# A gated mix of a long convolution and an MLP mixer: the DFT split 32 x 64 on halves of the PE array, with other transposes and another order of work

## The chip, the cores and the metric

The kernel runs on one core of one Trainium2 chip. The metric is the time of one execution on the device in microseconds (us): 305.72, the median of three runs (305.12 to 305.99). A core has TensorE (PE, with its weight loads as PEld), VectorE (DVE), ScalarE (ACT), GpSimd (POOL) and SyncE (SP), which here issues all DMAs. Each runs its own instructions in order and waits for the others at semaphores.

## The reference

Two branches over a sequence of S = 2048 rows of D = 640 channels, in bf16, mixed by a gate for each row. Branch A multiplies a 4-tap shifted k by v, convolves the product with a 2048-tap filter per channel, adds a direct term, and multiplies by q. Branch B is an MLP mixer on the same x (A_q): layer norm, w1, gelu, shifts of the four channel groups by +1, -1, +2, -2 rows, w2, a residual, layer norm, w3, gelu, w4, a residual.

```python
g = sigmoid((x * gate_w).sum(-1, keepdims=True))
k_shift = sum(k_pad[:, t:t + S, :] * shift_k[:, 3 - t] for t in range(4))
kv = k_shift * v
y = irfft(rfft(pad(kv, 2 * S)) * rfft(pad(ssm_k, 2 * S)))[:, :S] + kv * ssm_D
a = q * y
h = gelu(layernorm(x) @ w1)
x1 = x + shift_groups(h, (1, -1, 2, -2)) @ w2
b = x1 + gelu(layernorm(x1) @ w3) @ w4
out = g * a + (1 - g) * b
```

## The kernel before

**Layout.** A tile of 128 partitions holds the rows t = 16 t2 + t1 with t2 on the partitions and t1 = 0..15 as 16 slots of 640 channels. X (later X1, in place) and KV hold all 2048 rows in this way.

**Branch B.** `load_x` brings a quarter of x, `x_transpose` turns it with one DMA transpose of 20 blocks (L460), `x_stats` gets the norm, `mlp1` (L509, L510) does w1 and gelu for one slot into hr, which is laid out by channel group. `h_dma` then issues five DMA transposes for a quarter: one for each channel group (L516, into HT, padded by 16 columns) and one for the rest (L517, into HM0). `h_mixed` shifts HM0 into HM with four DMAs and small DVE copies. `w2` (L554) reads the shifted blocks, adds into X on DVE (L558) and squares on ACT (L560). `x1_norm` and a DMA transpose (L578) give x1t, `w3` (L596, gelu L597) and `w4` (L604) follow. w4 adds its PSUM to X1 on DVE; the four last ones write the result.

**Branch A.** `kv_load` and `kv_compute` (DVE, L432 to L438) form KV. `h_transpose` turns the filter ssm_k on PE into HT0. The DFT of length 4096 is done in steps. `step1` multiplies by F1 (128 x 256, its halves hf = 0, 1), 1024 columns a PSUM tile, evicted by ACT (L323) and written to the scratch S_h or S_x in DRAM. `gather` reads the scratch with rows and columns exchanged, `step2` multiplies by the table T2 (32 groups), `product` multiplies the two spectra on DVE (L357 to L359), `step3` multiplies by I1 and I2 and writes S_g, `gin` reads it back exchanged, and `step4` (L616) adds both halves of F4 and combines with q, the gate and X1 on DVE (L621 to L628). The tables T2, I1, I2 are spread out by POOL (L240) out of CMP. All evictions of step1, step2 and step3 are ACT's.

**What sets the order.** Every piece is put into a list with a time, and the list is sorted; up to time 45 the order of SP's instructions is that of the list, the rest is left to the scheduler of the framework. Pools limit what can run ahead: PSUM has two pools of two buffers, psc (branch A) and psm (branch B); hr, xn and a few others share two "row" buffers; HT0, the tables and W1N share one place (tag RT), W3 and the first part of ssm_k another.

Of the kernel before, what the change touches and what calls it, by code (L numbers as in the profile page):

```python
# [20 lines left out]
NT = 16  # L21
NG = 32
# [4 lines left out]
HS = 160  # L27
HPAD = 16
# [14 lines left out]
def kernel(  # L43
# [16 lines left out]
    nc = tc.nc  # L60
    V, A, G, PE, SP = nc.vector, nc.scalar, nc.gpsimd, nc.tensor, nc.sync

    q_rows = A_q.rearrange("b (t2 t1) d -> (b t2) t1 d", t1=NT)
    k_rows = A_k.rearrange("b (t2 t1) d -> (b t2) t1 d", t1=NT)
    v_rows = A_v.rearrange("b (t2 t1) d -> (b t2) t1 d", t1=NT)
    o_rows = out.rearrange("b (t2 t1) d -> (b t2) t1 d", t1=NT)
# [3 lines left out]
    PC = []  # L70
    n0 = 0
    for gi in range(4):
        PC.append((n0, 128, gi * 160))
        n0 += 128
    for gi in range(4):
        PC.append((n0, 32, gi * 160 + 128))
        n0 += 32

    tasks = []
    GTB = 4  # L80

    def add(t, fn):
        tasks.append((t, len(tasks), fn))
# [9 lines left out]
    S_h = [dram.tile([P, NT * D], BF16, name=f"S_h{i}") for i in range(2)]  # L93
    S_x = [dram.tile([P, NT * D], BF16, name=f"S_x{i}") for i in range(2)]
    S_g = [dram.tile([16, P, D], BF16, name=f"S_g{i}") for i in range(2)]
# [3 lines left out]
    F1 = const.tile([P, 256], BF16, name="F1")  # L99
    F4 = const.tile([P, 2, P], BF16, name="F4")  # L100
    CMP = const.tile([P, 3, NG, 2, 16], BF16, name="CMP")
# [3 lines left out]
    R128 = const.tile([P, P], F32, name="R128")  # L105
# [9 lines left out]
    EX = G  # L115
# [45 lines left out]
    def load_x(c):  # L161
        SP.dma_start(out=X[:, 4 * c:4 * c + 4, :], in_=q_rows[:, 4 * c:4 * c + 4, :])
# [6 lines left out]
    def load_w2():  # L169
        for (nn, cnt, oo) in PC:  # L170
            kt, po = nn // P, nn % P
            SP.dma_start(out=W2P[po:po + cnt, kt, :], in_=B_w2[oo:oo + cnt, :])
# [10 lines left out]
    def consts0():  # L183
        G.iota(pi[:], pattern=[[0, 1]], base=0, channel_multiplier=1)
        G.iota(R128[:], pattern=[[1, P]], base=0, channel_multiplier=0, allow_small_or_imprecise_dtypes=True)
# [558 lines left out]
```

## Time and profile before

| | |
|---|---|
| median of the runs | 305.72 us |
| the profiled execution | 304.15 us, span of its instructions 302.3 us |
| PE busy | 242.2 us, 80% of the span |
| PEld busy | 121.2 us |
| DVE busy | 176.9 us, 58% |
| ACT busy | 179.1 us, 59% |
| POOL busy | 28.3 us |
| DMA | 62.50 MB, mean 207 GB/s |
| granted clock of PE, mean | 0.941 |

The page gives busy time of an engine, its share of the span, and the same in 40 slices of 7.6 us, in tenths. Matmuls overlap, so that a run of them has to be read from the start of one to the start of the next. A row of the timeline gives start, length, engine, line, operation, what is written from what, the number of instructions put together, and in brackets how long the engine was idle ahead of it and for whom. A row of the grouped lines gives shapes and count, busy time, mean length in ns of one, then idle time and for whom. The rows of the stretches give, for PE, PEld, DVE, ACT and POOL, busy us and count, then the clock, the share of DMA and GB/s.

### The profile page before, as it was taken

The numbers are of one execution on the slowest core, as the hardware profiler recorded it, in microseconds if no ns is written. First come the engines' busy times: TensorE is split into PE (matmuls) and PEld (weight loads), VectorE is DVE, ScalarE is ACT, GpSimd is POOL, SyncE is SP. The second block draws the span as 40 slices with busy tenths as digits, with TensorE's granted clock in tenths as the row PEclk, the third lists the DMA queues.
The fourth block names the chain that finished last, engine by engine and source line by source line (L and its number), as shares of the span: only waits on it lengthen the run. The fifth ranks groups of instructions, "written<-read, shape, count | busy, mean of one in ns | idle before, by whom it ended". The sixth has DMA issues, their size and how long they took to land.

```text
span 302.3 us, 3944 instructions
## 1 busy us (share of the span) xinstructions
PE 242.2 (80%) x1434; PEld 121.2 (40%) x1434; DVE 176.9 (58%) x344; ACT 179.1 (59%) x284; POOL 28.3 (9%) x31
## 2 busy tenths in 40 slices
PE   2058858364639888999999999999999999995585
PEld 1024535231205444444454445444445454453232
DVE  8767969927899876501125234462343724099983
ACT  1999867242626666997868886469793676400000
POOL 6011302000000211990000000000000000000000
PEclk9999998975968999999999999999999999999559
DMA  6999979585699299958975458554975021775511
GB/s 201 242 259 401 206 202 314 96 236 170 157 283 400 59 269 280 359 205 225 321 288 173 129 193 194 183 173 128 413 242 174 3 87 43 245 278 175 175 43 43
DMA packets 60307, 62.50 MB, mean 207 GB/s; under 512 B 34304, under 2 KB 51457, under 8 KB 60288
## 3 DMA queue, kind: packets, MB, share of 16 engines
q1 hardware_dynamic: 60288, 62.25, 67.2%
q8 instruction: 11, 0.18, 0.2%
q14 instruction: 8, 0.07, 0.1%
HBM read 35.55 MB, written 18.35 MB: 178 GB/s over the span
## 4 chain that ended last, share of the span: by engine, by line
PE 30%; DVE 22%; ACT 13%; SPq 7%; DMA 7%; issue 6%; POOL 1%; ACTq 0%; DVEq 0%; POOLq 0%
PE ps L604 9%; PE ps L596 8%; ACT xs L348 6%; SPq L516 5%; PE ps L321 3%; DVE hs L359 3%; DVE p L358 3%; DVE p L357 3%; PE ps L370 3%; DVE X L558 3%; ACT gs L374 3%; DVE ot L625 2%; ACT stg L323 2%; PE ps L372 2%; PE ps L346 2%
## 5 line engine op out<-in xcount | busy, mean ns | idle before, releaser
L604 PE MATMUL ps<-W,gt 128*128 128x512 bf16 (+1 forms) x384 | 62.5, 306 | 0.8 <-DVE ot L607 0.8
L596 PE MATMUL ps<-x1t,W 128*128 128x512 bf16 x240 | 59.0, 379 | 0.0
L323 ACT CAST stg<-ps 128x1024 bf16<-128x1024 f32 x40 | 38.4, 1020 | 20.5 <-PE ps L321 10.4
L509 PE MATMUL psm<-WA,xt 128*128 128x512 bf16 (+1 forms) x160 | 30.0, 348 | 20.3 <-DVE WA L455 10.2
L604 PEld LDWEIGHTS <-gt 128*128 128x128 bf16 x384 | 30.2, 99 | 24.8 <-issue 3.7
L610 DVE TENSOR_TENSOR X<-ps,X 128x640 bf16<-128x640 f32 x12 | 9.9, 823 | 47.9 <-PE ps L604 47.9
L596 PEld LDWEIGHTS <-W 128*128 128x128 bf16 x240 | 22.3, 97 | 25.2
L357 DVE TENSOR_TENSOR p<-xs,hs 64x2560 bf16<-64x2560 bf16 x8 | 11.9, 1487 | 33.2 <-ACT xs L348 33.2
L374 ACT CAST gs<-ps 128x640 bf16<-128x640 f32 x32 | 20.6, 695 | 16.7 <-PE ps L372 14.5
L597 ACT ACTIVATE gt<-ps 128x1024 bf16<-128x1024 f32 x24 | 24.6, 1027 | 8.0 <-PE ps L596 7.7
L509 PEld LDWEIGHTS <-xt 128*128 128x128 bf16 x160 | 14.9, 111 | 32.0 <-issue 18.5
L346 PE MATMUL ps<-ax,TB 128*128 128x512 bf16 (+1 forms) x128 | 26.2, 298 | 0.3
L554 PE MATMUL psw<-WA,HT 128*128 128x512 bf16 (+1 forms) x128 | 22.4, 306 | 4.6 <-DVE X L558 3.6
L348 ACT CAST xs<-ps 128x640 bf16<-128x640 f32 x32 | 20.2, 696 | 9.0 <-PE ps L346 8.9
L321 PE MATMUL ps<-HT,F 128*128 128x512 bf16 x40 | 13.4, 441 | 13.9 <-ACT stg L323 7.2
L348 ACT CAST hs<-ps 128x640 bf16<-128x640 f32 x32 | 20.3, 696 | 0.1
L464 POOL TENSOR_TENSOR rs<-ve,EXPO 128x4 f32<-128x4 f32 x8 | 10.3, 1290 | 106.7 <-DVE ve L572 70.3
L437 DVE TENSOR_TENSOR acc<-acc,tmp 128x1280 bf16<-128x1280 bf16 x24 | 19.7, 823 | 0.5
L432 DVE TENSOR_TENSOR tmp<-K,cj 128x1280 bf16<-128x1280 bf16 (+1 forms) x25 | 19.8, 794 | 0.4
L510 ACT ACTIVATE hr<-psm,rs 128x640 bf16<-128x640 f32 x16 | 12.6, 807 | 12.4 <-DMA HM<-hr 5.9
L616 PE MATMUL ps<-gin,F 128*128 128x512 bf16 (+1 forms) x64 | 13.4, 347 | 7.4 <-DVE gq L622 6.7
L622 DVE TENSOR_TENSOR gq<-ps,gq 128x640 bf16<-128x640 f32 x16 | 12.6, 825 | 11.0 <-PE ps L616 11.0
(99 smaller groups left out, 309.0 us busy)
## 6 DMA issues: line engine op xcount, KB each, us to landing
S_h<-stg SPq DMA_DIRECT2D x10, 512.0 KB, 4.1
ax<-S_h SPq DMA_DIRECT2D x8, 640.0 KB, 4.2
S_x<-stg SPq DMA_DIRECT2D x10, 512.0 KB, 3.0
ax<-S_x SPq DMA_DIRECT2D x8, 640.0 KB, 4.7
S_g<-gs SPq DMA_DIRECT2D x16, 320.0 KB, 2.3
gin<-S_g SPq DMA_DIRECT2D x8, 640.0 KB, 7.8
W<-in_B_w_dram SPq DMA_DIRECT2D x2, 1920.0 KB, 9.3
X<-in_A_q_dram SPq DMA_DIRECT2D x4, 640.0 KB, 7.4
```

Of the source, the lines that this page charges most:

```text
L321: PE.matmul(ps[:, b * 512:(b + 1) * 512], lhsT=F1[:, hf * P:(hf + 1) * P], rhs=src[:, o:o + 512], start=True, stop=True)
L323: A.copy(out=stg[:, u * 1024:(u + 1) * 1024], in_=ps[:])
L346: PE.matmul(ps[:, o:o + w], lhsT=st["T2"][:, g, :], rhs=ax[:, i, o:o + w], start=True, stop=True)
L348: A.copy(out=dst[:, i, :], in_=ps[:])
L357: V.tensor_tensor(out=p2[0:64], in0=x[0:64], in1=h[64:128], op=ALU.mult)
L374: A.copy(out=gs[:, i % 2, :], in_=ps[:])
L432: V.tensor_tensor(out=dst[:, i:i + n, :], in0=K[:, r:r + n, :], in1=cj[:, j:j + 1, :].to_broadcast([P, n, D]), op=ALU.mult)
L509: PE.matmul(ps[:, o:o + w], lhsT=xt[:, i, k, :], rhs=W1X[:, k, o:o + w], start=(k == 0), stop=(k == DC - 1))
L554: PE.matmul(ps[:, o:o + w], lhsT=h_tile(f, t1), rhs=W2P[:, f, o:o + w], start=(f == 0), stop=(f == 4))
L596: PE.matmul(ps[:, u, :].rearrange("p (a b) -> p a b", a=4), lhsT=st["W3"][:, k, f * P:(f + 1) * P], rhs=xt[:, :, k, :], start=(k == 0), st ...
L597: A.activation(out=gt[:, 2 * (fp % 2):2 * (fp % 2) + 2, :], in_=ps[:], func=ACT.Gelu_apprx_tanh)
L604: PE.matmul(ps[:, o:o + w], lhsT=st["gt", c, f // 4][:, f % 4, i * P:(i + 1) * P], rhs=st["W4"][:, f, o:o + w], start=(f == 0), stop=(f == ...
```

## The change

The rows are now t = 32 t2 + 16 r + t1, with r on the two halves of the partitions (64 r + t2). The DFT is split 32 x 64: step1 is a product with a 64-row F1 for each r, on the upper or the lower rows of the PE array; step4 is a product with a 64-column F4 for each r, on the left or the right columns, with no sum over halves. Steps 2 and 3 keep their number and shape of matmuls. Every DMA between DRAM and such a tile becomes two of 64 rows. `h_dma` issues one transpose of 20 blocks for a quarter, and `h_shift` makes the shifted and wrapped blocks with small copies on DVE or POOL. X1 is multiplied by 1 - g ahead of w4 (`scale_x1`, on DVE or POOL), q by the gate ahead of step4 (`gate_q`), and the result is summed in X1 and written from there by `finish`. Some evictions of step1 to step3 go to DVE, 11 of 16 of step4 to ACT. The shift weights come as one row and are spread over the partitions by PE (`load_cj`, `kv_consts`). The order is written out as a list of names; SP's is fixed for the first 113 of them.

```diff
+H = 64
-    S_h = [dram.tile([P, NT * D], BF16, name=f"S_h{i}") for i in range(2)]
+    S_h = dram.tile([P, 2, NT * D], BF16, name="S_h")
...
+    def get_rows(dst, src):
+        for r in range(2):
+            SP.dma_start(out=dst[H * r:H * r + H], in_=src[r])
...
-        SP.dma_start(out=X[:, 4 * c:4 * c + 4, :], in_=q_rows[:, 4 * c:4 * c + 4, :])
+        get_rows(X[:, 4 * c:4 * c + 4, :], q_rows[:, :, 4 * c:4 * c + 4, :])
...
-        for (nn, cnt, oo) in PC:
-            kt, po = nn // P, nn % P
-            SP.dma_start(out=W2P[po:po + cnt, kt, :], in_=B_w2[oo:oo + cnt, :])
+        SP.dma_start(out=w[:, 0:4, :], in_=g[:, 0:128, :].rearrange("g p e -> p g e"))
+        SP.dma_start(out=w[:, 4, :], in_=g[:, 128:160, :])
...
-                PE.transpose(out=ps[:, i, :], in_=hv[:, 8 * hh + i, :], identity=IDB[:])
+                for r in range(2):
+                    PE.transpose(out=ps[H * r:H * r + H, i, :], in_=hv[:, 8 * hh + i, r], identity=IDB[:])
...
-            for b in range(2):
-                o = c * 2048 + u * 1024 + b * 512
-                PE.matmul(ps[:, b * 512:(b + 1) * 512], lhsT=F1[:, hf * P:(hf + 1) * P], rhs=src[:, o:o + 512], start=True, stop=True)
+            o = c * 1024 + u * 512
+            for r in range(2):
+                PE.matmul(ps[:, r, :], lhsT=F1[H * r:H * r + H, :], rhs=src[H * r:H * r + H, o:o + 512], start=True, stop=True)
...
-        for f in range(4):
-            SP.dma_start_transpose(out=st["HT"][:, f, 4 * c:4 * c + 4, HPAD:HPAD + P], in_=hr[:, f].rearrange("p a b -> p (a b)"))
-        SP.dma_start_transpose(out=st["HM0"][:, 4 * c * P:(4 * c + 4) * P].rearrange("p (a b) -> p a b", a=4), in_=hr[:, 4].rearrange("p a b -> p (a b)"))
+        SP.dma_start_transpose(out=st["HT"][:, 4 * c:4 * c + 4].rearrange("p a b c -> p (a b) c"), in_=hr[:].rearrange("p a b c -> p (a b c)"))
...
+    def h_shift(c, ev):
+        E = G if ev == "G" else V
+        for gi, s in enumerate(SHIFTS):
+            a = slice(32 * gi, 32 * gi + 32)
+            lo, hi = max(4 * c + s, 0), min(4 * c + 4 + s, NT)
+            E.tensor_copy(out=HM[a, lo:hi, :], in_=HT[a, lo - s:hi - s, 4, :])
+            if c == (3 if s > 0 else 0):
...
+                turn(E, HW[:, i:i + n, :], HT[:, u:u + n, gi, :], s)
+                turn(E, HM[a, w:w + n, :], HT[a, u:u + n, 4, :], s)
...
+    def scale_x1(t1, ev):
+        (G if ev == "G" else V).tensor_scalar(out=X1[:, t1, :], in0=X1[:, t1, :], scalar1=OMG[:, t1:t1 + 1], scalar2=0.0, op0=ALU.mult, op1=ALU.add)
+
+    def finish(t1):
+        if t1 in done:
+            for r in range(2):
+                SP.dma_start(out=o_rows[r, :, t1, :], in_=X1[H * r:H * r + H, t1, :])
+        done.add(t1)
...
-            V.tensor_tensor(out=X1[:, t1, :], in0=ps[:], in1=X1[:, t1, :], op=ALU.add)
+        V.scalar_tensor_tensor(out=X1[:, t1, :], in0=ps[:], scalar=OMG[:, t1:t1 + 1], in1=X1[:, t1, :], op0=ALU.mult, op1=ALU.add)
+        finish(t1)
...
-            for hf in range(2):
-                PE.matmul(ps[:, o:o + w], lhsT=F4[:, hf, :], rhs=st["gin", hf][:, t1 * D + o:t1 * D + o + w], start=(hf == 0), stop=(hf == 1))
+            for r in range(2):
+                PE.matmul(ps[H * r:H * r + H, o:o + w1], lhsT=F4[:], rhs=g[:, r, (t1 % 8) * D + o:(t1 % 8) * D + o + w1], start=True, stop=True)
...
+        if ev == "A":
+            A.copy(out=y[:], in_=ps[:])
+            V.tensor_tensor(out=y[:], in0=y[:], in1=q, op=ALU.mult)
+        else:
+            V.tensor_tensor(out=y[:], in0=ps[:], in1=q, op=ALU.mult)
+        V.tensor_tensor(out=X1[:, t1, :], in0=X1[:, t1, :], in1=y[:], op=ALU.add)
+        finish(t1)
...
-    tasks.sort(key=lambda e: (e[0], e[1]))
+    FIRST = 113
+    ORDER = (
+        "open.A2.right open.L1.left load_w1 consts0 load_cj load_x.0 load_x.2 x_stats.0.VVAA f1_table f4_table "
...
+    with tc.manual_schedule(engines={mybir.EngineType.SP}):
+        emit(ORDER[:FIRST])
+    emit(ORDER[FIRST:])
```

SP's queue in the first third, before, from the second quarter of h to the last; L516 and L517 are the transposes of hr, L172 the pieces of w2's weights, L417 and L419 the loads of k and v, L326 a write of step1:

```order
L460 DMA_TRANSPOSE xt<-X 128x20x128
L516 DMA_TRANSPOSE HT<-hr 128x4x128 x4
L517 DMA_TRANSPOSE HM_243<-hr 128x4x128
L172 DMA WA<-in_B_w_dram 128x640 x4
L172 DMA WA<-in_B_w_dram 32x640 x4
L417 DMA K<-in_A_k_dram 128x1280
L419 DMA KV<-in_A_v_dram 128x1280
L516 DMA_TRANSPOSE HT<-hr 128x4x128 x4
```

And now all four quarters of h (L537), behind the loads of k and v (L435, L86), with the filter's loads (L149) and w2's weights (L161, L162) between:

```order
L483 DMA_TRANSPOSE xt_329<-X 128x20x128 x2
L428 DMA K<-in_A_k_dram 63x1920
L435 DMA K<-in_A_k_dram 64x1280 x2
L537 DMA_TRANSPOSE HT<-hr 128x20x128
L149 DMA E<-in_A_ssm_k_dram 128x2048 x2
L537 DMA_TRANSPOSE HT<-hr 128x20x128
L161 DMA WA<-in_B_w_dram 128x4x640
L162 DMA WA<-in_B_w_dram 128x1x640
```

Twenty small transposes have become four large ones; step1's writes, which stood between them, now stand behind them, and ten half loads of k and v stand ahead of the first.

PE at step1 of KV, before, among w3 (L596), and now, among w4 (L644); ps_1215 and ps_1293 are PSUM tiles of step1:

```order
L596 MATMUL ps_1202<-x1t,W_876 128x512
L321 LDWEIGHTS F_79
L321 MATMUL ps_1215<-KV,F_79 128x512
L321 LDWEIGHTS F_79
L321 MATMUL ps_1215<-KV,F_79 128x512
L321 LDWEIGHTS F_79
```

```order
L644 MATMUL ps_1469<-W_1187,gt 128x512
L324 LDWEIGHTS F_76
L324 MATMUL ps_1293<-KV,F_76 128x512
L324 LDWEIGHTS F_76
L324 MATMUL ps_1293<-KV,F_76 128x512
L644 LDWEIGHTS gt
```

The two matmuls of a PSUM tile now use 64 rows of the array each; over the program there are 35 places where PE goes over from whole-array matmuls to such pairs and 35 where it goes back.

POOL, the whole of its work behind the norms' first powers, before (L464 powers, L240 tables), and now (L487 powers, L561 copies of `h_shift`, L628 `scale_x1`, L603 xn, L280 tables, L655 `gate_q`):

```order
L464 TENSOR_TENSOR rs_985<-ve,EXPO 128x4
L464 TENSOR_TENSOR rs_1343<-ve,EXPO 128x4
L464 TENSOR_TENSOR rs_1762<-ve,EXPO 128x4
L240 TENSOR_SCALAR TB<-CMP,sm 128x64x16 x4
L240 TENSOR_SCALAR TB<-CMP,sm 128x32x32 x8
```

```order
L487 TENSOR_TENSOR rs_1457<-ve,EXPO 128x4
L603 TENSOR_SCALAR xn<-X,m,rs_1457 128x640
L628 TENSOR_SCALAR X<-X,OMG 128x640 x3
L487 TENSOR_TENSOR rs_1735<-ve,EXPO 128x4
L603 TENSOR_SCALAR xn<-X,m,rs_1735 128x640 x2
L628 TENSOR_SCALAR X<-X,OMG 128x640 x3
L280 TENSOR_SCALAR TB<-CMP,sm 128x64x32 x2
L280 TENSOR_SCALAR TB<-CMP,sm 128x32x32 x4
```

The tables now stand behind pieces that were DVE's or did not exist, and DVE still has its convolution to do then.

More of the change, by code (lines that the diff above doesn't have):

```diff
@@ L26 @@
 SHIFTS = (1, -1, 2, -2)
-HS = 160
-HPAD = 16
 def pieces(width):
@@ L284, in tables @@
+        for c in range(2):
+            n = tab([P, NG, 32], "n")
+            ts(n[:], m[:], 2048.0 * (1 - c) + 4096.0, op0=ALU.add)
+            sin_table(CMP[:, 1, :, c, :], n, 8192)
     def tables():
@@ L338, in step2 @@
+    def step2(name, s, ev):
+        ax = st.pop((name, s))
         if name == "h":
```

425 lines of the change are left out of this document (179 added, 246 removed), and 27 rows, old and new, of the table ORDER.

## The prediction

> **What bounds the kernel now.** I read the busy tenths of the page first: PE is full only in the middle, and its clock sags where it is not.
>
> ```profile
> PE   2058858364639888999999999999999999995585
> DVE  8767969927899876501125234462343724099983
> PEclk9999998975968999999999999999999999999559
> ```
>
> A slice is 7.6 us. From slice 16 (121 us) to slice 34 (about 262 us) PE is at 9 tenths; there only the number and pace of matmuls count. Outside, 121 us ahead and 40 us behind, PE waits. So I ask of each part who is late there. Ahead, SP's queue, in order of time:
>
> ```profile
> 1.79 1.00 SPq L162 DMA_DIRECT2D X<-in_A_q_dram  x2
> 8.21 3.16 SPq L460 DMA_TRANSPOSE xt<-X  x1
> 28.09 4.74 SPq L460 DMA_TRANSPOSE xt<-X  x1
> 32.93 5.99 SPq L516 DMA_TRANSPOSE HT<-hr  x4
> 39.02 1.21 SPq L517 DMA_TRANSPOSE HM<-hr  x1
> 43.83 7.62 SPq L460 DMA_TRANSPOSE xt<-X  x1
> 51.54 5.92 SPq L516 DMA_TRANSPOSE HT<-hr  x4
> 58.81 3.86 SPq L172 DMA_DIRECT2D WA<-in_B_w_dram  x8
> 75.62 5.31 SPq L516 DMA_TRANSPOSE HT<-hr  x4
> 103.33 3.13 SPq L578 DMA_TRANSPOSE x1t<-xn  x1
> ```
>
> A DMA transpose holds SP's queue while it is issued, 1.3 us for a small one, and the five small ones of a quarter take 6.3 to 7.2 us. The last transpose of x is not issued until 43.8 us, the last ones of h not until 75.6 us, and w2 runs steadily only from 90.7 us, when DVE has copied the wrapped blocks of HM and worked off its convolution:
>
> ```profile
> 90.69 0.63 PE L554 MATMUL psw<-WA,HM 128*128 128x512 bf16 x1
> L432 DVE TENSOR_TENSOR tmp<-K,cj 128x1280 bf16<-128x1280 bf16 x23 | 18.9, 821 | 0.4
> ```
>
> Behind the middle, step4 waits for DVE, four DVE pieces for a tile pair, and four w4 tiles lie among and behind it:
>
> ```profile
> 263.45 0.50 PE ps L616 x3
> 267.04 0.68 DVE L621 TENSOR_SCALAR gq<-q,GS 128x640 bf16<-128x640 bf16 x2
> 267.63 1.55 DVE L622 TENSOR_TENSOR gq<-ps,gq 128x640 bf16<-128x640 f32 x2
> 269.10 1.68 DVE L625 SCALAR_TENSOR_TENSOR ot<-X,OMG,gq 128x640 bf16<-128x640 bf16 x2
> 289.85 8.76 PE ps L604 x48
> ```
>
> From 263.45 us to the end of the span are 38.9 us.
>
> **Part A, up to w2 (before: 90.7 us).** The sum goes along SP's new queue. xt.0 starts at 8.2 and holds 3.2; four half loads of X at 0.5 (two whole ones took 1.00) end at 13.4. xt.1 must wait for X.1, and such a load lands after 7.4:
>
> ```profile
> X<-in_A_q_dram SPq DMA_DIRECT2D x4, 640.0 KB, 7.4
> x1t<-xn SPq DMA_TRANSPOSE x4, 5.1
> ```
>
> So 19.3; xt.1 to xt.3 at 4.8 (about the middle of 3.2, 4.7 and 7.6 above) end at 33.7; ten half loads of K and v at 0.48 (eight W2 loads took 3.86) at 38.5. Then four transposes of h, each one instruction of 20 blocks, the form of x1t (3.1) and of xt (4.7): I take 4.0. Between them lie two loads of ssm_k, two of W2 and one more of ssm_k, 0.48 each. h.3 starts at 52.9 and lands 5.1 later, at 58; the shifted copies on DVE, some fourteen small ones that no row of this shape prices (I take 0.2, half of a 640-column xn), end near 61. I take **63**, two more for a full DMA. The bounds: all seven transposes behind xt.0 at 3.1 give 55, at 7.6 give 86. The doubled loads cost SP their 0.48 each and are in the sum. hr has two row buffers, so a quarter of mlp1 leaves PSUM only when the transpose two quarters back has landed:
>
> ```profile
> L510 ACT ACTIVATE hr<-psm,rs 128x640 bf16<-128x640 f32 x16 | 12.6, 807 | 12.4 <-DMA HM<-hr 5.9 <-PE psm L509 4.0 <-issue 1.6
> ```
>
> h.1 starts at 43.5 and lands at 48.6; four activations at 0.81 and the small copies of z behind them end by 52.6, just ahead of h.3: no further wait, but no slack either. Half of the PE transposes of ssm_k (82 of 160) stand behind the first w2 matmul and fill the wait for h.3.
>
> **Part B, up to the first step2.** Paces of PE from the full middle:
>
> ```profile
> 104.06 1.54 PE psw L554 x10
> 33.12 1.17 PE L304 MATMUL pst<-IDB,E 128*128 128x128 bf16 x16
> 128.52 2.16 PE ps L596 x10
> 130.68 0.86 PE ps L321 x4
> 153.56 3.26 PE ps L604 x24
> ```
>
> PE has 16 tiles of w2 at 1.38 (1.54 less the 0.16 by which the end of a run overlaps the next, below) = 22, 78 transposes at 0.07 = 5.5, 80 step1 matmuls at 0.215 = 17.2, 8.4 groups of w3 at 2.16 = 18.1, four tiles of w4 = 13.0: 75.7. DVE has from w2's first tile to the end of the convolution: 46 pieces of it at 0.82 = 38, 16 w2 tiles at 0.78 (as L622, also a product from PSUM) = 12.5, twelve xn at 0.38 and small ones 6.3, seven scale_x1 at 0.38 = 2.7, three w4 tiles 2.3, ten step1 evictions. These last no row shows; ACT's 0.695 for 640 columns (the row of gs in part C) scaled to 1024 gives 1.11, DVE's 0.78 gives 1.25; I take 1.15 since a copy reads one operand as ACT's does, 11.5. Sum 73. The other new thing is POOL, which now works beside the convolution:
>
> ```profile
> 107.86 1.51 DVE L575 TENSOR_SCALAR xn<-X,m,rs 128x640 bf16<-128x640 bf16 x4 [1.12 <-POOL rs L464]
> 122.23 3.92 DVE L575 TENSOR_SCALAR xn<-X,m,rs 128x640 bf16<-128x640 bf16 x4 [1.21 <-POOL rs L464]
> 122.44 13.45 POOL L240 TENSOR_SCALAR TB<-CMP,sm 128x1024 bf16<-128x1024 bf16 x12 [0.24 <-ACT stg L323]
> ```
>
> The same four pieces took 1.51 alone and 3.92 beside POOL's table: 0.6 lost for each us of POOL. Before, the table met almost nothing else on DVE. Now POOL has 13.4 of table, nine scale_x1 and four xn at about 0.7, 22.5 in all, and 62% of DVE's B is SBUF work of this kind: 22.5 x 0.62 x 0.6 = 8. So B is DVE's, **81**. The bounds are 73 (no loss) and 95 (all 22.5).
>
> The Trainium skill (SBUF — State Buffer, section SBUF: two separate sides) says that VectorE and GpSimd share a port pair as an exclusive lock, held for a whole instruction, for VectorE work in a two-port mode or with two SBUF inputs. The rows of xn agree. By the rule alone DVE would lose up to all of POOL's time; that is the rival on POOL below.
>
> Packing: a pair of 64-row step1 matmuls may run at once, 8.6 less than 17.2. Against it stand the changes between half and whole array: the new order has 70 of them around step1. What one costs no row shows. Two matmuls alone among others start 0.43 ahead of the next one and end after 0.59:
>
> ```profile
> 147.69 0.59 PE L321 MATMUL ps<-KV,F 128*128 128x512 bf16 x2
> 148.12 0.59 PE L604 MATMUL ps<-W,gt 128*128 128x512 bf16 x2
> ```
>
> If a change waits for that end, 70 x 0.16 = 11. The two bounds, -8.6 and +11, cancel about; I keep step1 at 17.2, and since DVE is later in B the gain would be hidden there anyway.
>
> The Trainium skill (TensorEngine Tiling (Array Packing), Key Properties) says that a change of tiling mode drains the TensorE while separate tiles run in parallel. By it PE's B would be 67 to 78; no run shown yet can tell.
>
> **Part C, the rest of the full middle.** PE has 15.6 groups of w3 (33.7), 12 tiles of w4 (39.1), step2 and step3 as before, 128 tiles of four or two matmuls at 0.27 a pair, 34.6: 107.4; PE is busy 98% in this stretch, which makes 109:
>
> ```profile
> 160.00:180.00 20.00, 19.61 (x107) 9.10 (x105) 8.59 (x6) 17.07 (x25) 0.00 (x0) 1.00 0.56 173
> 256.70 2.27 DMA S_g<-gs
> ```
>
> All four late w4 tiles are now ahead of step4, and the last writes of S_g and loads of gin (from 256.7 to 263.45 before) hide behind 11 us of these. DVE has 40 evictions at 0.7 to 0.78, the products at 1.49 and 12 w4 tiles:
>
> ```profile
> L357 DVE TENSOR_TENSOR p<-xs,hs 64x2560 bf16<-64x2560 bf16 x8 | 11.9, 1487 | 33.2 <-ACT xs L348 33.2
> L374 ACT CAST gs<-ps 128x640 bf16<-128x640 f32 x32 | 20.6, 695 | 16.7 <-PE ps L372 14.5 <-ACT gs L374 2.2
> ```
>
> 30 + 36 + 10 + 2 = 78 of 109: not the bound in sum. I take **108**, the middle of the two.
>
> **Part D, step4.** ACT now evicts 11 of 16 tiles (7.7 in all, beside DVE). DVE has 5 products from PSUM at 0.78, 11 products and 16 additions in SBUF at 0.42 (half of the 0.82 for 1280), five gate_q at 0.34, one w4 tile: 17.6. Two rings of q refill inside the tail and each costs about 1.5 of waiting on DVE (load lands 3 after its issue, issued behind the outputs). Start 0.6; last output 2.8, as now. **23** to 26 against 38.9. SP issues 32 outputs at 0.48, 15 us, beside it. If packing fails here, PE's 16 tiles take 8.6 instead of 4.3, both below DVE's 17.6.
>
> **Sum.** 63 + 81 + 108 + 23 = 275 of span. The profiled execution took 304.15 with a span of 302.3, so 1.85 lies around it: **277**. The median of the runs, 305.72, is 1.6 above the profiled one, within what the range holds.
>
> **Rivals.** (1) *All goes well*: packing gives its 8.6, changes cost little, POOL and DVE miss each other: B 70, A 61, rest as above, 264. For: the middle of the trace shows PE at 98% with the same kind of order. (2) *A is the DMA's, not SP's*: the share of DMA is above 1 in rows of 12 to 40 us:
>
> ```profile
> 12.00:17.00 5.00, 0.00 (x0) 0.10 (x1) 3.99 (x9) 5.00 (x12) 0.00 (x0) 1.00 1.09 205
> 33.00:40.00 7.00, 6.78 (x69) 4.68 (x67) 6.87 (x13) 6.98 (x14) 0.51 (x1) 1.00 1.05 129
> ```
>
> If the transposes hold SP half-way to the worst of 7.6 (6 each), A is 75 and the time 289. Against: less is loaded ahead of w2 (no broadcast of the shift weights, no early q). (3) *POOL shuts DVE out* for all its 22.5: B 95, time 291. (4) *The change doesn't pack*: pairs run one behind the other and every change drains: PE's B is 75.7 + 11 = 87, time 283. (5) *Slower*: evictions that all went to ACT now stand on DVE's queue behind products and convolution. PE has two buffers; if each of the 50 DVE evictions of step1 to step3 holds PE for one product (1.49), 75 us come on top: 352. It decides at 28/50 = 0.56 us each: above that the kernel is slower than before. For: DVE's queue is in order, and PE's too. Against: DVE is at 70% in C, and w3 and w4 use another pair of buffers, so that PE has work until its next turn.
>
> **Chances.** Forecast (270 to 285) 0.40; (1) 0.25; (2) 0.13; (3) 0.10; (4) 0.05; (5) 0.07. The range 263 to 294 holds forecast, (2) to (4) and most of (1). Only (5) ends at or above the old time: faster by over 0.3% 0.92, within 0.3% (about what a measurement of this kernel can tell) 0.01, slower 0.07.
>
> **What would show it.** Right: w2's first matmul near 63 us, PE at 9 tenths from there, its clock at full where it sagged; step2's first matmul near 144; step4's first near 252, DVE back to back behind it. Convolution pieces of DVE longer than 0.82 beside POOL show the port; matmul starts of step1 pairs 0.43 apart show no packing, gaps around them the drain. Wrong: w2 later than 75, or PE waiting in C for evictions on DVE.

## The result and the profile after

| | before | changed |
|---|---|---|
| median of 4 runs each, us | 305.42 (304.48 to 305.99) | 297.09 (295.73 to 297.51) |
| ratio to before, 95% interval | | 0.9722 (0.9679 to 0.9765) |
| profiled execution: time / span, us | 304.15 / 302.3 | 297.50 / 295.7 |
| first steady w2 matmul, us | 90.7 | 62.9 |
| first step2 matmul | 149.5 | 149.3 |
| first step4 matmul | 263.45 | 264.1 |
| from there to the end | 38.9 | 31.6 |

The kernel is faster, by 8.3 us and not by 28. The same three strips of the page as before (a slice is now 7.4 us):

```profile
PE   2375929789999999878999999999999999957220
DVE  7699699359899999999335996885878855319193
PEclk9999886999999999989999999999999999985555
```

PE is at 7 tenths or more from slice 6 (44 us) to slice 34: w2 starts 27.8 us earlier. But neither step2 nor step4 starts earlier to speak of, and behind step4 stand four slices in which PE's clock is at half. So the 27.8 us are gone between w2 and step4, and of the tail only 7.3 us are saved. Part of the 27.8 is work that was moved: of the 384 matmuls of w4, 96 more than before (four tiles, 13 us) and 78 of the PE transposes (5 us) now stand in that stretch. The forecast counted these. Where the rest went shows when it is set against the forecast, stage by stage (all by the profiled execution; 260.9 is 264.10 less the wait of 3.23 in the row below):

| stage | forecast | measured | difference |
|---|---|---|---|
| A, up to w2 | 63 | 62.9 | -0.1 |
| B and C, w2 to the last w4 matmul ahead of step4 | 81 + 108 | 198.0 | +9.0 |
| PE waits for gin | 0 | 3.2 | +3.2 |
| D, step4 to the end | 23 | 31.6 | +8.6 |
| span | 275 | 295.7 | +20.7 |

More than half of it lies at the end. The timeline of SP's queue in the changed kernel (start, duration, what is issued, how many):

```profile
250.84 0.54 SPq L387 DMA_DIRECT2D gin<-S_g  x1
251.79 0.36 SPq L381 DMA_DIRECT2D S_g<-gs  x1
252.21 7.41 SPq L387 DMA_DIRECT2D gin<-S_g  x4
266.26 6.71 SPq L636 DMA_DIRECT2D out_dram<-X  x10
273.08 2.21 SPq L86 DMA_DIRECT2D q<-in_A_q_dram  x2
275.39 3.74 SPq L636 DMA_DIRECT2D out_dram<-X  x6
279.23 1.18 SPq L86 DMA_DIRECT2D q<-in_A_q_dram  x2
282.91 10.37 SPq L636 DMA_DIRECT2D out_dram<-X  x16
```

And from the chain that ended last, PE's timeline and DVE's, what waited for these (in brackets the idle time ahead of an instruction and what ended it):

```profile
251.79 5.93 DMA S_g<-gs
257.81 6.25 DMA gin<-S_g
264.10 1.28 PE L664 MATMUL ps<-gin,F 128*64 128x512 bf16 x8 [3.23 <-DMA gin<-S_g]
279.53 1.23 DVE L655 TENSOR_SCALAR q<-q,GS 128x640 bf16<-128x640 bf16 x2 [6.17 <-DMA q<-in_A_q_dram]
290.43 0.49 DVE L672 TENSOR_TENSOR X<-X,y 128x640 bf16<-128x640 bf16 x1
```

Three things are to be seen. The last write of S_g and the loads of gin behind it take 12.3 us, and of the late w4 tiles only 9.1 us are left to cover them (251.8 to 260.9). The refill of q is issued behind ten outputs, 0.67 us each, and DVE stands still for 6.2 us. And the last sixteen outputs, 0.65 each, are issued until 293.3, 2.4 us after DVE's last piece. All of these are SP's and the DMA engines', and of all three the forecast had said that they lie beside other work or cost little.

### The profile page after: what moved, and what is told of

Same layout as the page of the kernel before. It is cut to its first block, busy times and chain, and to the rows that moved or that the text cites. A ratio compares the mean times of both kernels' runs of the same rounds, so it can differ in the third digit from the quotient of the medians.

```text
span 295.7 us, 4202 instructions
## 1 busy us (share of the span) xinstructions
PE 238.4 (81%) x1496; PEld 120.6 (41%) x1519; DVE 221.8 (75%) x425; ACT 152.5 (52%) x235; POOL 59.9 (20%) x48
## 4 chain that ended last, share of the span: by engine, by line
DVE 31%; PE 31%; DMA 19%; SPq 6%; issue 6%; ACT 6%; DVEq 0%; ACTq 0%
PE ps L624 8%; DMA HT<-hr 7%; PE ps L644 5%; PE ps L349 5%; PE psm L531 3%; PE psw L582 3%; DVE acc L455 3%; DMA ax<-S_h 3%; PE ps L373 3%; DVE p L361 3%; DMA X<-in_A_q_dram 2%; DVE tmp L450 2%; DVE hs L362 2%; DVE xs L353 2%; DVE X L586 2%
## 5 line engine op out<-in xcount | busy, mean ns | idle before, releaser
L644 PE MATMUL ps<-W,gt 128*128 128x128 bf16 (+1 forms) x375 | 59.5, 300 | 0.5 <-issue 0.2
L531 PE MATMUL psm<-WA,xt 128*128 128x129 bf16 (+1 forms) x157 | 28.4, 348 | 15.5 <-ACT ZG L533 10.2
L644 PEld LDWEIGHTS <-gt 128*128 128x128 bf16 x384 | 29.1, 99 | 23.1 <-issue 2.7
L326 ACT CAST stg<-ps 128x1024 bf16<-128x1024 f32 x30 | 29.4, 1020 | 11.4 <-DMA S_h<-stg 4.5
L655 POOL TENSOR_SCALAR q<-q,GS 128x640 bf16<-128x640 bf16 x6 | 5.5, 921 | 134.1 <-DMA q<-in_A_q_dram 134.1
L531 PEld LDWEIGHTS <-xt 128*128 128x128 bf16 x160 | 15.0, 112 | 29.7 <-issue 15.9
L487 POOL TENSOR_TENSOR rs<-ve,EXPO 128x4 f32<-128x4 f32 x8 | 9.5, 1192 | 72.7 <-DVE ve L600 23.0
L668 ACT CAST y<-ps 128x640 bf16<-128x640 f32 x11 | 7.4, 693 | 30.4 <-PE ps L664 15.1
L377 ACT CAST gs<-ps 128x640 bf16<-128x640 f32 x20 | 13.5, 696 | 18.5 <-PE ps L375 18.2
L664 PE MATMUL ps<-gin,F 128*64 128x512 bf16 (+1 forms) x64 | 10.8, 465 | 14.5 <-ACT y L668 10.2
L645 DVE SCALAR_TENSOR_TENSOR X<-ps,OMG,X 128x640 bf16<-128x640 f32 x16 | 14.1, 880 | 9.9 <-PE ps L644 9.9
L353 DVE CAST hs<-ps 128x640 bf16<-128x640 f32 x15 | 11.9, 820 | 10.2 <-PE ps L349 10.2
L351 ACT CAST xs<-ps 128x640 bf16<-128x640 f32 x19 | 12.7, 693 | 12.5 <-issue 7.2
L349 PEld LDWEIGHTS <-TB 128*128 128x128 bf16 x128 | 11.9, 97 | 14.9 <-issue 4.2
```

The source lines that it names most:

```text
L326: A.copy(out=stg[:, :, u * 512:(u + 1) * 512], in_=ps[:])
L349: PE.matmul(ps[:, o:o + w], lhsT=st["T2"][:, g, :], rhs=ax[:, i, o:o + w], start=True, stop=True)
L353: V.tensor_copy(out=dst[:, i, :], in_=ps[:])
L377: A.copy(out=gs[:, i % 2, :], in_=ps[:])
L531: PE.matmul(ps[:, o:o + w], lhsT=xt[:, i, k, :], rhs=W1X[:, k, o:o + w], start=(k == 0), stop=(k == DC - 1))
L644: PE.matmul(ps[:, o:o + w], lhsT=st["gt", c, f // 4][:, f % 4, i * P:(i + 1) * P], rhs=st["W4"][:, f, o:o + w], start=(f == 0), stop=(f == ...
```

## The experiments

Times are medians; the ratio is to the kernel before, run on the same chip. The last column is what the ratio says against the changed kernel: (ratio - 0.9722) x 305.4 us.

| run | us | ratio (95%) | against changed |
|---|---|---|---|
| e1_q_early | 295.24 | 0.9635 (0.9586 to 0.9684) | -2.7 |
| e5_gin_manual | 297.00 | 0.9709 (0.9663 to 0.9755) | -0.4 |
| e10_pair_out | 293.82 | 0.9618 (0.9578 to 0.9657) | -3.2 |
| e11_all_tail | 289.89 | 0.9480 (0.9447 to 0.9514) | -7.4 |
| e12_gin_by_tile | 285.73 | 0.9340 (0.9303 to 0.9377) | -11.7 |
| e2_step1_act | 297.57 | 0.9710 (0.9660 to 0.9760) | -0.4 |
| e3_no_pool | 299.46 | 0.9774 (0.9731 to 0.9817) | +1.6 |
| e4_small_transposes | 302.45 | 0.9895 (0.9858 to 0.9932) | +5.3 |
| e6_kv_later | 305.09 | 0.9979 (0.9951 to 1.0007) | +7.8 |
| e7_c_act | 293.11 | 0.9584 (0.9540 to 0.9628) | -4.2 |
| e13_tail_c_act | 286.39 | 0.9355 (0.9321 to 0.9389) | -11.2 |
| e8_same_half | 300.82 | 0.9859 (0.9811 to 0.9908) | +4.2 |
| e14_step1_whole | 296.82 | 0.9700 (0.9649 to 0.9752) | -0.7 |

### The tail: q, gin and the outputs

**q early.** The last two quarters of q go where W3 stood, which is free once the last w3 is done.

```diff
-        q2 = ring.tile([P, 4, D], BF16, name="q2", tag="row", bufs=2)
+        if c < 2:
+            q2 = ring.tile([P, 4, D], BF16, name="q2", tag="row", bufs=2)
+        else:
+            if c == 2:
+                st["q23"] = main.tile([P, 2, 4, D], BF16, name="q23", tag="W3")
+            q2 = st["q23"][:, c - 2]
...
-"w3.3.5 w4.15"
+"w3.3.5 load_q.2 load_q.3 w4.15"
```

> Edit: the third and fourth quarter of q get rows of their own (where W3 stood) and are loaded ahead of step4, not inside it. Theory (the tail waits 8.6 us on DVE for the two refills of q): from step4's first matmul to the end 31.6 falls to 23 to 26, and the time by 6 to 8.6 us, to 288.5 to 291. Rival (the tail's pace is DVE's and POOL's sum; the refill only shows a wait that another takes over): less than 3 us, 294 to 297.

2.7 us: the rival. DVE was done early, but the end did not follow. DVE's last piece and SP's row of outputs in this run:

```profile
282.61 0.88 DVE L677 TENSOR_TENSOR X<-X,y 128x640 bf16<-128x640 bf16 x2
263.63 28.34 SPq L636 DMA_DIRECT2D out_dram<-X  x32
```

DVE ends at 283.5 instead of 290.9, 7.4 us earlier, as the theory had it for DVE. But SP issues its 32 outputs until 292.0. The wait for q had hidden a wait for SP's queue. In that row SP itself waits, by the profile, 4.9 us for loads of gin to land and 2.5 us for loads of q, so the late loads are part of it; why an output waits for them is not shown.

**The written order around the last write of S_g.** No load of gin's second half (gin.1) goes ahead of the last write.

```diff
-    emit(ORDER[FIRST:])
+    a = ORDER.index("gin.0.96.128")
+    emit(ORDER[FIRST:a])
+    with tc.manual_schedule(engines={mybir.EngineType.SP}):
+        emit(ORDER[a:a + 6])
+    emit(ORDER[a + 6:])
```

> Edit: SP keeps the written order around the last writes of S_g, so that no load of gin.1 is issued ahead of the last write, and gin.0.96.128 is the first load behind it. Theory (the 3.23 us of PE ahead of step4 are the last write's late landing, 5.9 instead of 2.3, plus four gin loads that share the queue): step4 starts at 261 or just behind, the time falls by 2.5 to 3.5 us. Rival (the tail waits for q and the outputs anyway, so an earlier start is waited out at the first refill): less than 1 us.

No change: the rival again, though its reason was only half of it. PE's timeline:

```profile
259.90 0.73 PE L664 MATMUL ps<-gin,F 128*64 128x512 bf16 x8
271.63 1.27 PE L664 MATMUL ps<-gin,F 128*64 128x512 bf16 x8 [6.09 <-DMA out_dram<-X]
```

Step4 starts 4.2 us earlier. But its ninth tile, the first of gin's second half, starts at 271.63, in the changed kernel at 271.65. (The profile puts the 6.09 us down to an output DMA; the tile reads gin.1, and in the chain that ended last of this run the last load of gin is issued at 255.8 and lands 15.6 us later, as in e11 below.) The refill of q is issued at 273.25, for 273.08 in the changed kernel, so the earlier start is waited out.

**Outputs two tiles at a time.**

```diff
-            for r in range(2):
-                SP.dma_start(out=o_rows[r, :, t1, :], in_=X1[H * r:H * r + H, t1, :])
+            full.add(t1)
+            a = t1 - t1 % 2
+            if a in full and a + 1 in full:
+                for r in range(2):
+                    SP.dma_start(out=o_rows[r, :, a:a + 2, :], in_=X1[H * r:H * r + H, a:a + 2, :])
```

> Edit: the output is written two neighbouring tiles at a time, 16 DMAs of 160 KB instead of 32 of 80 KB; nothing else. Theory (SP's queue sets the tail: 32 issues at 0.63 us, ten of them ahead of the refill of q and sixteen behind the last tiles): q's refill is issued 3 us earlier and the last outputs end nearer to DVE's last piece, so the time falls by 4 to 7 us. Rival (the tail is DVE's work plus the landing of q; the outputs only fill SP's free time): less than 1.5 us.

3.2 us, between the two. The refill of q is issued at 270.7 instead of 273.1, and the last output 1.1 us behind DVE's last piece instead of 2.4. So the count of output DMAs, doubled by the two halves r, has a price: 16 instead of 32 save some 3 us of the tail.

**All three together.**

> Edits together: q in rows of its own and early, the written order around the last write of S_g, and outputs two tiles at a time. Theory (tail = gin wait, then q's refill, then SP's issues, each hiding behind the next): step4 starts at 260 to 262, DVE works 19 to 22 us from there, and the last output is issued within 2 us of DVE's end: 284 to 288 us. Rival (landing of DMAs in the tail, not their issue, is the bound: 2.6 MB of gin, 0.7 MB of q and 2.6 MB of output share the engines): 291 to 295.

289.89, between again: 7.4 us are gained where the single edits gave 2.7, 0.4 and 3.2. One wait is left, in the chain that ended last:

```profile
256.39 15.93 DMA gin<-S_g
272.45 0.76 PE ps L672 x4
```

The last load of gin.1 is issued at 256.4 and lands 15.9 us later. The four loads of gin.1, gin.0's last one, q and the first outputs are under way at once, and each tile of the second half needs all four, since a load brings 32 partitions of all eight tiles.

**gin.1 tile by tile**, in the order in which step4 uses the tiles, with step4's order made to fit.

```diff
+        if q == 1:
+            for t in range(a // 16, b // 16):
+                SP.dma_start(out=st["gin", q][:, :, t * D:(t + 1) * D], in_=S_g[:, :, (8 + t) * D:(9 + t) * D])
+            return
...
-gin.1.0.32 gin.1.64.96 gin.1.32.64 gin.1.96.128
+gin.1.64.96 gin.1.0.32 gin.1.32.64 gin.1.96.128
...
-"step4.13.A w4.13 step4.8.A step4.10.A step4.11.V step4.12.A gate_q.9.G step4.9.V step4.15.A step4.14.A"
+"step4.13.A w4.13 step4.12.A gate_q.9.G step4.8.A step4.9.V step4.10.A step4.11.V step4.15.A step4.14.A"
```

> Edit on top of the three tail edits: gin of the second half is loaded tile by tile (eight loads of 128 partitions, in the order in which step4 uses the tiles) in place of four loads of 32 partitions that all eight tiles need. Theory (in the tail PE waits 6.6 us for the last of four gin loads, 15.9 us after its issue, because all four share the DMA engines and every tile needs all four): the first tiles come 4 to 8 us after the last write of S_g, the 6 us gap goes, and the time falls to 284 to 287 from 289.9. Rival (smaller rows of 1280 bytes cost the DMA engines what the order gains): 289 to 293.

285.73, as the theory had it, and the fastest version here: 0.934 of before. Its step4:

```profile
261.13 0.73 PE L676 MATMUL ps<-gin,F 128*64 128x512 bf16 x8 [0.25 <-DMA gin<-S_g]
279.58 0.49 DVE L684 TENSOR_TENSOR X<-X,y 128x640 bf16<-128x640 bf16 x1
```

The span ends at 284.9: 23.8 us from step4's first matmul, with DVE at work nearly all of the time up to 280.1. That is the forecast's part D (23) to within 1 us, but partly by luck. The forecast's 23 had room for two waits for q, which are gone here. DVE's own work came out right, 17.1 us for 17.6; what follows its last piece takes 4.8 us, where the forecast had 2.8. Missing from the sum was what DVE waits for. The loads by tile and their new order were not tried apart.

### The stretch from w2 to step4

**ACT takes DVE's evictions of step1** (each of the ten V in the step1 names of the order becomes A).

> Edit: all 40 evictions of step1 on ACT, ten of them taken off DVE (about 12 us of DVE ahead of the first step2). Theory (the stretch from w2 to the first step2 is DVE's): the last convolution piece ends 6 to 10 us earlier, and the time falls by 4 to 9 us. Rival (PE's count bounds the stretch from w2 to step4, with only 8 us of idle in it): the convolution ends earlier, but the time falls by at most 4 us, or not at all.

The time does not move, as the rival said, but neither did the convolution end earlier, which both had expected: its last piece starts at 138.00 instead of 138.21. Three rows of this run say why (SP, then DVE):

```profile
109.49 8.46 SPq L606 DMA_TRANSPOSE x1t<-xn  x1
126.81 1.54 SPq L435 DMA_DIRECT2D K<-in_A_k_dram  x2
131.32 0.82 DVE L450 TENSOR_TENSOR tmp<-K,cj 128x1280 bf16<-128x1280 bf16 x1 [2.36 <-DMA K<-in_A_k_dram]
```

The last piece of K is issued by SP behind transposes of x1 and writes of S_h, and DVE, which has caught up, waits for it. PE's waits for step1's evictions only changed the engine: 3.5 us for DVE and 1.0 for ACT in the changed kernel, 3.2 for ACT here. So this run does not tell whether DVE's work or PE's bounds B; it shows that SP's queue is right behind DVE.

**POOL's share of x1 and xn on DVE** (each G in the names scale_x1 and x1_norm becomes V).

> Edit: scale_x1 and xn off POOL onto DVE (13 pieces of 0.38 us, 5 us more for DVE); POOL keeps the tables and gate_q. Theory (POOL beside DVE costs DVE more than the pieces themselves): convolution pieces fall from 0.93 to about 0.85, the tables start earlier, and the time falls by 1 to 4 us. Rival (POOL is the side that loses; DVE is hardly slowed): DVE ends 3 to 5 us later in that stretch, and the time stays within 1 us or rises by up to 4.

About 1.6 us slower, but the intervals overlap; a gain of 1 to 4 us, as in the theory, is not there. The pieces of the convolution, which the theory saw fall to 0.85 us, stay where they were (929 ns before this edit):

```profile
L455 DVE TENSOR_TENSOR acc<-acc,tmp 128x1280 bf16<-128x1280 bf16 x24 | 22.1, 922 | 0.3
```

So the pieces of x1 and xn on POOL had cost DVE next to nothing. The rival's end of DVE, 3 to 5 us later, did not come either: the last piece of the convolution ends at 138.8 instead of 139.9.

**K and v later on SP**, behind the last transpose of h.

```diff
-x_transpose.3 kv_load.0 kv_load.1 kv_consts.VVV
+x_transpose.3 kv_consts.VVV
...
-h_dma.3 h_shift.3.V
+h_dma.3 kv_load.0 kv_load.1 h_shift.3.V
```

> Edit: the ten half loads of K and v that stand ahead of the first transpose of h on SP (6.2 us) are put behind the last one. Theory (SP's queue sets the first part, and from w2 on PE's own sum is the bound, so that an earlier w2 is carried to the end): w2 starts 4 to 6 us earlier and the time falls by 3 to 6 us. Rival (the convolution, which then starts later, holds up DVE and so the first step2): w2 starts earlier, but PE waits more ahead of step2 and the time falls by less than 2 us or rises.

7.8 us slower, the rival and more. w2 runs steadily from 54.9, 8 us earlier; the convolution starts at 58.4 instead of 34.4. The windows from 100 to 140 us of this run and of the changed kernel (busy time of PE, PEld, DVE, ACT, POOL; then PE's clock, the share of DMA, GB/s):

```profile
100.00:120.00 20.00, 11.29 (x46) 3.58 (x46) 19.07 (x32) 8.21 (x10) 12.06 (x8) 0.81 0.83 262
120.00:140.00 20.00, 16.96 (x100) 7.16 (x100) 19.93 (x27) 8.54 (x9) 17.79 (x9) 0.94 0.72 187
```

```profile
100.00:120.00 20.00, 19.24 (x98) 7.77 (x98) 20.00 (x34) 12.15 (x14) 11.30 (x6) 1.00 0.97 281
120.00:140.00 20.00, 16.03 (x83) 6.89 (x84) 19.86 (x22) 10.15 (x11) 19.89 (x11) 0.91 0.73 224
```

With the convolution late, PE runs out of work in the window from 100 us and its clock falls to 0.81. Its longest wait there, 6.0 us, ends at 114.85, when DVE has just finished a piece of KV (114.75) that step1 reads. So in B DVE's chain does bound PE as soon as it is later than in the changed kernel. There PE idles 4 us, in the window from 120 us, 3.2 of them for evictions of step1 in DVE's queue. The two chains end nearly together.

**Small transposes of h**, which undoes one part of the change.

```diff
-        SP.dma_start_transpose(out=st["HT"][:, 4 * c:4 * c + 4].rearrange("p a b c -> p (a b) c"), in_=hr[:].rearrange("p a b c -> p (a b c)"))
+        for i in range(4):
+            SP.dma_start_transpose(out=st["HT"][:, 4 * c + i], in_=hr[:, i].rearrange("p b c -> p (b c)"))
```

> Edit: each quarter of h goes through four DMA transposes of 5 blocks instead of one of 20. Theory (SP's queue sets the first part; a small transpose holds it for 1.3 us, so a quarter takes 5.2 instead of 4.4, and w2's first steady matmuls come 2 to 5 us later): time up by 1 to 5 us. Rival (ahead of w2 the DMA engines are full, the share is 1.0 to 1.1, and the form of the transposes does not matter): w2 within 1 us, time within 1 us.

5.3 us slower, the theory, at the upper end of its range. SP's first two quarters in this run, and in the changed kernel:

```profile
36.16 6.33 SPq L538 DMA_TRANSPOSE HT<-hr  x4
43.68 5.52 SPq L538 DMA_TRANSPOSE HT<-hr  x4
```

```profile
35.66 4.82 SPq L537 DMA_TRANSPOSE HT<-hr  x1
41.69 4.80 SPq L537 DMA_TRANSPOSE HT<-hr  x1
```

1.5 and 0.7 us more for these two; w2's steady run comes 2.5 us later (65.82 against 63.35, the first matmul with a shifted tile HW), and all that SP issues behind it, the next K first (62.6 against 59.3).

**All evictions of step2 and step3 on ACT** (each V in their names becomes A).

> Edit: all 96 evictions of step2 and step3 on ACT, none on DVE (28 to 30 moved, about 20 us more for ACT). Theory (in the full middle PE's own sum is the bound and the evictions are hidden on either engine): within 1.5 us. Rival (evictions on DVE that stand behind products hold PE, the slower case of the forecast): the time falls by 3 us or more. Third (ACT's gelus of w3 and the evictions get in each other's way): up by 2 us or more.

4.2 us faster, which looks like the rival. But PE's timeline from 140 us to step4 shows hardly fewer waits (1.8 us of idle against 2.0). What moved is the order that the scheduler made of it: the last step3 matmuls come at 243, with 16 us of w3 and w4 behind them instead of 10, and the last write of S_g, issued at 251.79 in the changed kernel, is this one:

```profile
244.20 0.41 SPq L381 DMA_DIRECT2D S_g<-gs  x1
```

Step4 starts at 259.83 with no wait for gin. If that is the whole gain, it must vanish on top of the tail edits:

> The four tail edits with all evictions of step2 and step3 on ACT. Theory (that edit alone gained 4 us because the last write of S_g then came 6 us earlier and the load of gin was hidden behind w4, not because evictions held PE): with the tail edits, which have taken that wait already, it adds at most 1.5 us, 284 to 286. Rival (evictions on DVE held PE in the middle): the 4 us add, 281 to 283.

286.39 against 285.73: it adds nothing. Evictions on DVE did not hold PE.

### Halves of the array

**Same half**: both matmuls of a step1 pair read the lower 64 rows. **Whole array**: both read all 128.

```diff
-                PE.matmul(ps[:, r, :], lhsT=F1[H * r:H * r + H, :], rhs=src[H * r:H * r + H, o:o + 512], start=True, stop=True)
+                PE.matmul(ps[:, r, :], lhsT=F1[H:P, :], rhs=src[H:P, o:o + 512], start=True, stop=True)
...
+                PE.matmul(ps[:, r, :], lhsT=F1[:], rhs=src[:, o:o + 512], start=True, stop=True)
```

> Both matmuls of each step1 pair read the lower 64 rows, so that a pair cannot run at once; the result of the first pair member is that of the other half, which changes the output; counts of instructions and DMAs are the same. Theory (pairs do run at once: 0.54 us for four against 0.86): step1's 80 matmuls take 17 to 18 us of PE instead of 13.1, and the time rises by 2 to 5 us, as PE's sum bounds the stretch from w2 to step4. Rival (the pace of step1 is set by its evictions or there is no packing): within 1 us.

> Both matmuls of each step1 pair use all 128 rows (sums of the two halves, which changes the output); as many instructions, but no pair can overlap and none changes the form of the array. Theory (the change between half and whole array costs time): step1's 80 matmuls take 16.5 to 18 us of PE, 3 to 5 less than the 21.1 of two matmuls on the same half, and the difference over 70 changes is the price of one, 0.04 to 0.07 us; time up by 1 to 4 us against the changed kernel. Rival (changes are free, and what step1 takes beyond its matmuls are waits for its evictions): 20 to 22 us, as on the same half.

One pair of step1 between matmuls of w2, in PE's timeline of the changed kernel, of e8 and of e14. What counts is the distance from one start to the next:

```profile
77.03 0.38 PE L582 MATMUL psw<-WA,HT 128*128 128x512 bf16 x1
77.34 0.39 PE L324 MATMUL ps<-HT,F 64*128 64x512 bf16 x2
77.66 0.61 PE L582 MATMUL psw<-WA,HT 128*128 128x512 bf16 x2
```

```profile
76.22 0.38 PE L582 MATMUL psw<-WA,HT 128*128 128x512 bf16 x1
76.54 0.60 PE L324 MATMUL ps<-HT,F 64*128 64x512 bf16 x2
77.07 0.61 PE L582 MATMUL psw<-WA,HT 128*128 128x512 bf16 x2
```

```profile
76.00 0.60 PE L582 MATMUL psw<-WA,HT 128*128 128x512 bf16 x2
76.44 0.59 PE L324 MATMUL ps<-HT,F 128*128 128x512 bf16 x2
76.87 0.38 PE L582 MATMUL psw<-WA,HT 128*128 128x512 bf16 x1
```

On the whole array a 512-column matmul takes 0.22 and a pair 0.43. On one half twice, the pair takes 0.53, and the matmul ahead of it 0.32 instead of 0.22: 0.10 us for the change into halves and 0.10 for the change back. On two halves the pair takes 0.32, one matmul and one change: it does run at once. In sum a lone pair costs 0.42, changes included, and saves nothing against 0.43; only where two pairs follow each other (0.54 in the changed kernel, and 0.10 ahead) are 0.2 us saved. Over all 80 matmuls, from start to start in the timelines, step1 takes 13.1 us in the changed kernel, 21.1 in e8 and 18.2 in e14. The first two lack the 35 changes into halves, 3.5 us, which the timeline charges to the matmul ahead. So 16.6 against 18.2: the halves save PE 1.6 us, and in the time no gain shows (e14 is at -0.7 us, with intervals that overlap almost wholly). Without the overlap, 4.2 us are lost. e8's theory had the time right, but step1 took 21.1 us and not 17 to 18: it gave the changes no price. e14's put a change at 0.04 to 0.07 us, too low, and so expected e14 to be slower than the changed kernel, which it is not.

## Why the prediction was wrong

**Direction: right. Part A: right, its number partly by luck.** w2 came at 62.9 for 63, and SP's queue, the step that was named, does move it: e4 by the transposes alone, e6 by the loads ahead of them. But single terms miss on both sides. The transposes of x behind the first held SP for 3.0 to 3.5 us, not 4.8, and the first of h was issued at 35.7 for 38.5. Then came a wait that the forecast ruled out ("no further wait"): ACT stood until the transpose of h's first quarter, h.0, had landed, and h.2 and h.3 were issued 1.7 and 1.3 us after SP was free. And h.3, issued at 55.2 for 52.9, landed 7.4 us later instead of 5.1, while the 5 us for the shifted copies and a full DMA hardly appeared. ACT's row, and the chain that ended last:

```profile
42.29 0.79 ACT L532 ACTIVATE hr<-psm,rs 128x640 bf16<-128x640 f32 x1 [6.70 <-DMA HT<-hr]
49.55 13.10 DMA HT<-hr x2
```

The rival that A is the DMA engines' loses by e4, which moves the same bytes and is later; the longer landings are its share.

**Part D: wrong, +8.6, at its sentence "Two rings of q refill inside the tail and each costs about 1.5 of waiting on DVE (load lands 3 after its issue, issued behind the outputs)".** The first wait measured 6.2, the second nothing. The load landed 6.4 us after its issue (273.08 to 279.5 for both halves), not 3, and "issued behind the outputs" was given no price, where ten outputs at 0.67 stand. The second failed sentence is "SP issues 32 outputs at 0.48, 15 us, beside it". They took 0.65 each, 20.8 us, and not all beside DVE's work: ten stand ahead of q, and some behind the last piece. By the rows, D's 31.6 us are 0.8 up to DVE's first piece (forecast 0.6), 19.9 of DVE's work with short waits in it (17.6), 6.2 for q (3) and 4.8 behind DVE's last piece (2.8). The forecast's own terms give 24.0, of which it took 23. A third thing had no term at all: gin's second half, which the forecast took as loaded. In the changed kernel it costs nothing (the ninth tile waits 0.78 us, for an eviction); it shows once the other waits are gone, as 6.6 us of PE in e11. e12 takes the waits away, and D measures 23.8.

**The wait for gin: wrong, +3.2, at "the last writes of S_g and loads of gin (from 256.7 to 263.45 before) hide behind 11 us of these".** The cover was there, 10.2 us of w4 (9.1 of them behind the last write's issue), but the chain under it was never added up: 5.9 for the write (2.5 in e11, where no load of gin.1 is issued ahead of it) and 6.25 for the load. Both durations had near rows in the profile of before (2.3 and 7.8 in its table of DMA issues).

**Parts B and C: wrong in size, +9.0.** Some 1.5 of these are waits: between 62.9 and 260.9 PE idles 7.4 us in waits of over 0.15 us, where the forecast left it 5.9 (81 + 108 less PE's own 75.7 + 107.4). The other 7.4 are PE's own pace. By starts in the timeline, w3 took 56.7 us (forecast 24 groups at 2.16: 51.8), w4 55.9 (16 at 3.26: 52.1), step2 and step3 36.1 (34.6), w2 23.6 (22), transposes 5.2 (5.5), step1 13.1 (17.2): 190.6 for 183.2. The step that failed is "Paces of PE from the full middle": it took the longest undisturbed runs. The mean pace stood in the trace of before. Busy time of w3's and of w4's matmuls in it, by the windows view of their lines:

```profile
91.00:264.00 173.00, 58.96 (x240) 22.32 (x240) 1.00 0.63 207
91.00:264.00 173.00, 46.12 (x288) 22.05 (x288) 1.00 0.63 207
```

0.246 and 0.160 a matmul, where a run of ten in 2.16 and of 24 in 3.26 gives 0.216 and 0.136. The busy times count the overlapped ends, up to 0.16 at each piece. By starts, as above, w3 took 55.8 us before and the twelve tiles of w4 42.2, which is 56.3 for sixteen: 112.1 for both, as good as the 112.6 of the changed kernel, where the forecast had 103.9. In the changed kernel the 3.5 us of changes into halves are in the matmuls ahead of step1, of w2, w3 and w4; step1's own 13.1 for 17.2 makes up for them.

**B's inner working: half right.** DVE worked back to back up to 141 us, as forecast; but step2 came at 149.3, not 144, since behind the last eviction stand a gather and its landing, which the sum of B left out (the chain that ended last, and PE's timeline):

```profile
141.06 8.07 DMA ax<-S_h
149.27 0.70 PE L349 MATMUL ps<-ax,TB 128*128 128x512 bf16 x4 [0.71 <-DMA ax<-S_h]
```

PE had w3 and w4 to do meanwhile, so that this cost little.

**POOL: the step "8" measured about 4, and its rate of 0.6 holds for the table alone.** The largest group of the convolution in the table of groups, before and after (count, busy time, mean ns):

```profile
L437 DVE TENSOR_TENSOR acc<-acc,tmp 128x1280 bf16<-128x1280 bf16 x24 | 19.7, 823 | 0.5
```

```profile
L455 DVE TENSOR_TENSOR acc<-acc,tmp 128x1280 bf16<-128x1280 bf16 x24 | 22.3, 929 | 0.3
```

This group loses 2.6 us, the last step of KV (L456) 0.8, the multiplications of K (23 at 862 for 821) 0.9. Nearly all of it, 3.9 us, is lost by the four pieces that ran beside POOL's table (L280), 1.3 to 2.5 us each; the fifteen that ran beside x1 and xn lose some 0.6 us together. One of the four, and the table:

```profile
134.68 2.48 DVE L455 TENSOR_TENSOR acc<-acc,tmp 128x1280 bf16<-128x1280 bf16 x1
131.44 14.45 POOL L280 TENSOR_SCALAR TB<-CMP,sm 128x2048 bf16<-128x2048 bf16 x8
```

The forecast had read its rate from a table and put it on x1 and xn too. There POOL is the loser: a piece of x1 takes 0.80 us alone and 2.0 beside the convolution (three in 6.13), one of xn 3.8 (two in 7.56):

```profile
83.47 0.80 POOL L628 TENSOR_SCALAR X<-X,OMG 128x640 bf16<-128x640 bf16 x1 [0.64 <-DVE xn L603]
113.59 6.13 POOL L628 TENSOR_SCALAR X<-X,OMG 128x640 bf16<-128x640 bf16 x3
121.01 7.56 POOL L603 TENSOR_SCALAR xn<-X,m,rs 128x640 bf16<-128x640 bf16 x2
```

The Trainium skill (SBUF — State Buffer, section SBUF: two separate sides) says that VectorE and GpSimd share a port pair as an exclusive lock and that the loser blocks. The rows agree that one of them waits; which one depends here on POOL's piece, and why is not shown. The rival that POOL shuts DVE out for all its time is refuted: some 4 us are lost while POOL is busy for 40 (62.9 to 141.1).

**Packing: right, for the reason given.** The two bounds, -8.6 for overlap and +11 for 70 changes, were said to cancel about. The overlap is there, a change costs 0.10 and not 0.16 us, and what is left, 1.6 us of PE, does not show in the time (e14: -0.7 us without either). The rival that the change doesn't pack was half true: the changes cost nearly what the pairs save. The Trainium skill (TensorEngine Tiling (Array Packing), Key Properties) says that a change of mode drains the TensorE and that tiles run in parallel. The second holds here, two matmuls in 0.32 us with a change; of the first the rows show a price, 0.10 us a change, and not the drain itself.

**The slower rival: refuted.** In C PE waited 0.4 us for evictions on DVE and 0.9 for products, and e13 shows that moving all of them gains nothing. In B it waited 3.5 us for step1's evictions on DVE, and e2, which takes them off DVE, gains nothing.

What stays open: why PE's mean pace is longer than that of its longest runs. In e14, which has no changes into halves in step1, w3 and w4 still take 109.8 us by starts for the forecast's 103.9. These 6 us, perhaps the joins between short pieces of other kinds, were not tried alone.

## What to carry to other kernels

Add up the tail of a kernel by its DMAs first: each load and write on the last chain with its issue, its place in the issuing queue and its landing, and only then the engines' work; here DVE's own work was right to 1 us (17.1 for 17.6 in e12), and taking its waits for transfers and SP's queue away gained 11.7. Where several waits hide behind each other, removing one shows little (0.4 to 3.2 us each) and all of them together show their worth, so a small gain from one edit says nothing about the wait it removed. In step1, with 512 columns, halves of the PE array pay only where several pairs follow each other. And paces for a sum of PE are taken from means over the stretch, not from its best runs.

## What the runs showed of the hardware that was not expected

- A change between half and whole array costs 0.10 us each way, so a lone pair of 64-row matmuls with 512 columns saves nothing (0.42 against 0.43 us).
- One DMA transpose of 20 blocks held SP's queue for 3.0 to 4.8 us early on (those of h 3.8 to 4.8), and for 8.46 us in e2 at 109 us: for that long nothing behind it is issued.
- Beside POOL's table four pieces of the convolution took 1.3 to 2.5 us instead of 0.82; beside x1 and xn on POOL they took 0.81 to 0.95 with one exception (1.34), while a piece of x1 on POOL took up to 3.2 us instead of 0.80.
- With four loads of 640 KB issued one behind the other in e11, the last landed 15.9 us after its issue, where the median of such loads in the changed kernel is 6.2.
- In the tail PE's clock was granted at 0.5 to 0.6; with the waits gone (e12) it was 0.72 from 260 to 280 us.
